# Second-layer weights of a mixture-of-experts kernel: the low part written by ScalarE and finished by an adding DMA

## The chip, the cores and the metric

The kernel runs on one core of a Trainium2 chip. The metric is the device time in microseconds (us) of one execution. Before the change it is 1175.32 us, the median of 3 runs (1174.71 to 1176.95).

The core has five engines with queues of their own that meet only at semaphores. TensorE (PE) multiplies matrices, VectorE (DVE), ScalarE (ACT) and GpSimd (POOL) do elementwise work, SyncE (SP) issues DMAs. GpSimd's queue can issue DMAs too. All DMAs of the core run on the same 16 DMA engines.

## The reference

Three stages, one after the other, on 2304 tokens of 512 features. In short:

```python
x = attention(q, k, v)                    # 4 x 8 heads, 576 positions, local and strided masks
# first mixture: each token goes to one of 8 experts, at most 288 tokens an expert
for e in range(8):
    h = np.maximum(x[mask_e] @ w1[e], 0.0)
    out[mask_e] = h @ w2[e]
# second mixture: all 4 experts on every token, weighted by p
for e in range(4):
    h = np.maximum(x @ v1[e], 0.0)
    y += p[:, e:e + 1] * (h @ v2[e])
```

`w1` and `v1` are the first-layer weights (512 x 1024 for an expert), `w2` and `v2` the second-layer weights (1024 x 512). The experts of the first mixture are filled greedily, in the order of the gate's logits, which the kernel finds by a search.

## The kernel before, in words

Every product is taken three times: a number is split into a high part (rounded to fp32r) and a low part (what the rounding left), and the kernel adds high x high, high x low and low x high. So each weight needs a high tile `wh` and a low tile `wl = raw - wh`.

The program has three stages: attention (to about 140 us of the profiled execution), the routing stage (`steps`, to about 660 us), in which the eight routed experts and a part of the second mixture run interleaved while the search for the next expert's tokens goes on beside them, and the rest of the second mixture (`fast`, to the end). The change touches the routing stage alone.

The weights of the routing stage come in 136 chunks of 128 hidden columns. A chunk has two halves: a = 0 holds 512 x 128 of the first layer, a = 1 holds 128 x 512 of the second layer; each is 128 partitions x 512 floats (256 KB). A chunk passes these places:

- `load` (L841, L842): SP's queue issues one DMA per half into a `raw` tile. There are 8 such tiles, so 4 chunks; a tile is taken again when its last reader is done. SP's queue is in order.
- `prep_hi` (L867): ACT casts both halves to `wh`, some 4 steps ahead of the chunk's first use. `wh` and `wl` have slots for 8 chunks.
- `split_lo` (L875): one subtraction per half writes `wl`. It is recorded under L769 where DVE does it, since DVE's calls pass through a helper there, and under L875 where POOL does it: POOL takes the second halves of chunks 1 to 7 and some of the last chunks, when the search (`chains`) is over.
- `l1` and `l2` (L994): a step is 12 matmuls of the first layer, and 6 or 12 of the second layer, which come two steps later (`LK`). In between, ACT writes `hh = relu(h)` (L887), and DVE writes `hl` (L889, under L769).

The order of instructions is fixed when the program is built. A model called `Pace` counts the time of PE and of DVE; `fill` puts a subtraction of `split_lo` into the program where the model finds DVE free, and `tick` puts the next piece of the search (`chain_a`) or of the gather (`chain_b`) where its inputs should be there. So what DVE has to do decides where these pieces stand in the order of every engine. GpSimd's queue also issues the gathers of the tokens, `xg` (L914), and the scatters of finished rows, `out_dram` (L1090); both wait for DVE.

Of the kernel before, what the change touches and what calls it, by code (L numbers as in the profile page):

```python
# [22 lines left out]
AF = mybir.ActivationFunctionType  # L23
OP = mybir.AluOpType
# [715 lines left out]
NRAW = 4  # L740
# [32 lines left out]
def experts(tc, ident, hot, K, L, xd, side, w1, w2, v1, v2, out, hold, deferred):  # L773
    nc = Pace(tc.nc)
    D, F = 512, 1024
    with ExitStack() as st:
# [22 lines left out]
        for s, S in enumerate(steps):  # L799
            c = chunks[S["ch"]]  # L800
            c.setdefault("first", s)
            c["last"] = s
        for k, c in enumerate(chunks):
            lo = chunks[k - NSLOT]["last"] + 2 + LK if k >= NSLOT else 0
# [3 lines left out]
        plain = len(chunks)  # L808
# [4 lines left out]
        R = [dict() for _ in range(8)]  # L813
        done_l1 = [False] * 8
        state = {"load": 0, "prep": 0, "lo": 0}
# [12 lines left out]
        def load(k):  # L828
            c = chunks[k]
            raw = c["raw"] = [mp.tile([128, 512], FT, name="raw", bufs=2 * NRAW) for _ in range(2)]  # L830
            fc = c["fc"]
            if "m1" in c:
                g = c["m1"]
                ev = ereg[g]
                s1 = w1[bass.ds(ev, 1), :, fc * 128:fc * 128 + 128].rearrange("o (c p) f -> p (o c) f", p=128)
                s2 = w2[bass.ds(ev, 1), fc * 128:fc * 128 + 128, :].rearrange("o p d -> p (o d)")
            else:
                e = c["e"]
                s1 = v1[e, :, fc * 128:fc * 128 + 128].rearrange("(c p) f -> p c f", p=128)
                s2 = v2[e, fc * 128:fc * 128 + 128, :]  # L840
            nc.sync.dma_start(raw[0].rearrange("p (c f) -> p c f", c=4), s1)  # L841
            nc.sync.dma_start(raw[1], s2)  # L842

        def loads(need, ahead):
            while state["load"] < len(chunks):
                k = state["load"]
                c = chunks[k]
                if k >= need and k >= state["prep"] + ahead:
                    return
                if "m1" in c and c["m1"] not in ereg:  # L850
                    g = c["m1"]
                    if k >= need and "e" not in R[g]:
                        return
                    until(lambda: "e" in R[g])
                    ereg[g] = nc.sync.value_load(R[g]["ei"], min_val=0, max_val=7)
                load(k)
                state["load"] += 1

        def prep_hi(k):
            loads(k + 1, 0)  # L860
            c = chunks[k]
            c["at"] = nc.pe
            c["h"] = mp.tile([128, 1024], FR, name="wh", bufs=NSLOT)
            c["l"] = mp.tile([128, 1024], FR, name="wl", bufs=NSLOT)
            for a in range(2):
                sl = slice(512 * a, 512 * a + 512)
                nc.scalar.copy(c["h"][:, sl], c["raw"][a])  # L867

        def split_lo(pool=False):

            k, a = divmod(state["lo"], 2)
            c = chunks[k]
            sl = slice(512 * a, 512 * a + 512)
            eng = nc.gpsimd if pool or 0 < k < 8 and a or not chains and (a or k % 2) else nc.vector
            eng.tensor_tensor(c["l"][:, sl], c["raw"][a], c["h"].bitcast(FT)[:, sl], OP.subtract)  # L875
            state["lo"] += 1
            if a and "x" in R[0]:
                loads(0, NRAW)

        def fill():  # L880

            while chains and state["lo"] < 2 * min(plain, state["prep"]) and nc.dve <= nc.pe and chunks[state["lo"] // 2]["at"] + HI <= nc.pe:
                split_lo()
# [104 lines left out]
        def until(f):  # L988
            while not f():
                assert chains  # L990
                tick(0.1, "b" in chains)
# [156 lines left out]
        def preps(s, n=None):  # L1148
            while state["prep"] < (n or plain) and chunks[state["prep"]]["prep"] <= s:
                prep_hi(state["prep"])  # L1150
                state["prep"] += 1
            while state["lo"] < 2 * state["prep"]:
                c = chunks[state["lo"] // 2]
                if c["first"] > s + (1 if chains else 0) and (chains or c["prep"] >= s):
                    break
                split_lo()
# [177 lines left out]
        for k in range(PRE):  # L1334
            prep_hi(k)
            state["prep"] += 1
            for a in range(2):
                split_lo(a and k)
# [25 lines left out]
def attention_moe_moe(ctx, tc, q, k, v, wg, w1, w2, dp, v1, v2, out):  # L1364
    nc = tc.nc
    ctx.enter_context(tc.manual_schedule())
    cp = ctx.enter_context(tc.tile_pool(name="c", bufs=1))
    dr = ctx.enter_context(tc.tile_pool(name="dr", bufs=1, space=bass.MemoryType.DRAM))
    ident = cp.tile([128, 128], FT, name="ident")
    hot = cp.tile([128, 512], BF, name="hot")  # L1370
    nc.vector.memset(hot, 1.0)
    make_identity(nc, ident)
    L = cp.tile([128, 18, 8], FT, name="L")
    xd = dr.tile([2304, XW], FT, name="xd")
    side = dr.tile([2304, 8], FT, name="side")
    K = route_consts(nc, cp)
    yp = ctx.enter_context(tc.tile_pool(name="yp", bufs=1))
    ready = (lambda *a: first_best(nc, K, L, *a), lambda *a: first_reach(nc, K, *a), lambda *a: first_count(nc, K, *a))
    hold = lambda: yp.tile([128, 2304], FT, name="hold", bufs=3)
    deferred = []  # L1380
    front(tc, ident, hot, q, k, v, wg, dp, xd, L, ready, hold, deferred)
    experts(tc, ident, hot, K, L, xd, side, w1, w2, v1, v2, out, hold, deferred)
# [26 lines left out]
```

## Time and profile before

| | before |
|---|---|
| median of 3 runs | 1175.32 us |
| profiled execution, its own time | 1175.08 us |
| its span, first to last instruction | 1173.4 us |
| PE busy | 1145.3 us (98%) |
| DVE busy | 837.0 us (71%) |
| ACT busy | 613.8 us (52%) |
| POOL busy | 427.0 us (36%) |
| mean granted clock of TensorE | 0.993 |

An engine's busy time is the time in which one of its instructions ran, and it is a sum over stages with different limits: which engine sets the time is read stage by stage. A busy PE is not PE at its peak, since matmuls overlap. The profiled execution took 1.7 us more than its span, and its own time lies 0.24 us under the median, inside the spread of the runs.

### The profile page before, as it was taken

The page shows a single profiled execution, that of the slowest core. Times are in us where ns is not written, and L with a number is a line of the kernel's source. Part 1 is how long each engine was busy: PE and PEld are TensorE (multiplying, and loading weights), DVE is VectorE, ACT ScalarE, POOL GpSimd, SP SyncE. Part 2 cuts the span into 40 slices and gives each one's busy share as a digit, 9 for nine tenths or more (in the row PEclk, how much of TensorE's full clock was granted, in tenths as well). Part 3 has the DMA queues.
Part 4 walks back from the last instruction along what each step waited for, and adds up shares of the span by engine and source line. Part 5 has one row for each costly group of instructions (what it writes and reads, how often), then busy time and mean ns, then how long its engine had stood idle before and what let it go on. Part 6 is the DMA issues. An engine that isn't in the chain of part 4 may idle for free.

```text
span 1173.4 us, 24536 instructions
## 1 busy us (share of the span) xinstructions
PE 1145.3 (98%) x8845; PEld 1027.8 (88%) x8852; DVE 837.0 (71%) x2253; ACT 613.8 (52%) x1599; POOL 427.0 (36%) x474
## 2 busy tenths in 40 slices
PE   9999799999999999999999999999999999999997
PEld 6876598898998998999999999999898899899996
DVE  6777688787876887867755577776776776676663
ACT  5997455452442433555544555555555555555552
POOL 6453130001001000101105465556756566656652
PEclk9999899999999999999999999999999999999999
DMA  7881665553351533656565333333423333333320
GB/s 179 189 189 18 192 211 160 176 147 91 115 176 55 175 118 93 216 180 203 170 192 181 98 101 104 94 108 102 133 91 108 109 91 108 127 108 106 93 73 36
DMA packets 203387, 152.96 MB, mean 130 GB/s; under 512 B 42584, under 2 KB 169886, under 8 KB 202978
## 3 DMA queue, kind: packets, MB, share of 16 engines
q1 hardware_dynamic: 198946, 140.91, 41.0%
q0 software_dynamic: 4320, 10.49, 2.8%
q8 instruction: 69, 1.13, 0.4%
q14 instruction: 52, 0.43, 0.1%
HBM read 141.77 MB, written 9.58 MB: 129 GB/s over the span
## 4 chain that ended last, share of the span: by engine, by line
PE 81%; DVE 4%; ACT 4%; DMA 3%; issue 3%; POOL 3%; POOLq 0%; SPq 0%; ACTq 0%; DVEq 0%
PE o L994 37%; PE h L994 17%; PE h L1226 9%; PE pa L1226 7%; PE pb L1226 3%; DMA raw<-in_moe_w_dram 3%; ACT pr L213 2%; DVE wl L769 2%; POOL wl L1213 1%; PE pa L620 1%; PE pt L230 1%; POOL out_dram L1090 1%; PE s L194 1%; PE av L250 1%; PE tr L158 1%
## 5 line engine op out<-in xcount | busy, mean ns | idle before, releaser
L769 DVE TENSOR_TENSOR wl<-raw,wh 128x512 fp32r<-128x512 f32 x352 | 269.5, 795 | 5.2 <-ACT wh L867 1.8
L887 ACT ACTIVATE hh<-h 128x256 fp32r<-128x256 f32 (+1 forms) x256 | 100.1, 391 | 269.4 <-PE h L994 196.3
L994 PE MATMUL o<-wh,hh 128*128 128x512 f32 x576 | 226.8, 394 | 1.0 <-ACT y L1072 0.5
L994 PE MATMUL o<-wl,hh 128*128 128x512 f32 x576 | 226.5, 393 | 0.0
L994 PE MATMUL o<-wh,hl 128*128 128x512 f32 x576 | 226.0, 392 | 0.0
L1213 POOL TENSOR_TENSOR wl<-raw,wh 128x512 fp32r<-128x512 f32 x96 | 122.3, 1295 | 197.1 <-ACT wh L1212 165.4
L867 ACT CAST wh<-raw 128x512 fp32r<-128x512 f32 x272 | 160.0, 619 | 61.3 <-DMA raw<-in_moe_w_dram 59.5
L769 DVE SCALAR_TENSOR_TENSOR hl<-h,hh 128x256 fp32r<-128x256 f32 (+1 forms) x256 | 110.0, 430 | 114.5 <-ACT hh L887 113.6
L914 POOL DMA_INDIRECT xg<-xd,idx x24 | 27.7, 1152 | 330.4 <-DVE idx L769 194.5
L994 PEld LDWEIGHTS o<-wh,hl 128*128 128x128 f32 x576 | 108.3, 188 | 23.1
L994 PEld LDWEIGHTS o<-wh,hh 128*128 128x128 f32 x576 | 108.3, 188 | 7.2 <-ACT y L1072 0.7
L994 PEld LDWEIGHTS o<-wl,hh 128*128 128x128 f32 x576 | 108.4, 188 | 5.7
L769 DVE TENSOR_TENSOR wl<-sums,wh 128x512 fp32r<-128x512 f32 x96 | 82.1, 856 | 28.6 <-ACT wh L1199 28.5
L1199 ACT CAST wh<-sums 128x512 fp32r<-128x512 f32 x96 | 59.7, 623 | 81.0 <-POOL sums L1187 57.8
L994 PE MATMUL h<-xh,wh 128*128 128x288 f32 x256 | 76.2, 298 | 0.3 <-ACT xh L891 0.3
L994 PE MATMUL h<-xh,wl 128*128 128x288 f32 x256 | 75.7, 296 | 0.6 <-DVE wl L769 0.6
L994 PE MATMUL o<-hh,wl 128*128 128x288 f32 x256 | 76.2, 298 | 0.0
L994 PE MATMUL o<-hh,wh 128*128 128x288 f32 x256 | 76.1, 297 | 0.0
L994 PE MATMUL h<-xl,wh 128*128 128x288 f32 x256 | 75.8, 296 | 0.1
L994 PE MATMUL o<-hl,wh 128*128 128x288 f32 x256 | 75.5, 295 | 0.0
L994 PE MATMUL h<-y256h,wl 128*128 128x256 f32 x256 | 73.5, 287 | 0.0
L994 PE MATMUL h<-y256l,wh 128*128 128x256 f32 x256 | 73.2, 286 | 0.0
(318 smaller groups left out, 2920.0 us busy)
## 6 DMA issues: line engine op xcount, KB each, us to landing
raw<-in_moe_w_dram SPq DMA_DIRECT2D x464, 256.0 KB
vl<-in_v_dram SPq DMA_DIRECT2D x16, 192.0 KB
ql<-in_q_dram SPq DMA_DIRECT2D x12, 144.0 KB
kl<-in_k_dram SPq DMA_DIRECT2D x12, 144.0 KB
qs<-in_q_dram SPq DMA_DIRECT2D x2, 576.0 KB
ks<-in_k_dram SPq DMA_DIRECT2D x2, 576.0 KB
xd<-y SPq DMA_DIRECT2D x2, 576.0 KB
xd<-hl SPq DMA_DIRECT2D x5, 192.0 KB
```

What stands on the lines that cost most here:

```text
L158: nc.tensor.transpose(p[:, 72 * a:72 * a + 72], src[:, r:r + 2, :].rearrange("p r d -> p (r d)"), ident[:72, :72])
L194: nc.tensor.matmul(out[:rows], lt, rt, start=True, stop=True)
L213: nc.scalar.activation(e[:rows, j, :keys], T["s"][:rows, j, :keys], AF.Exp, scale=-1.0, bias=T["mx"][:rows, j:j + 1], accum_out=T["su"][:r ...
L230: nc.tensor.transpose(p[:keys, rows * j:rows * j + rows], T["p"][:rows, j, :keys], ident[:rows, :rows])
L769: return f(*args, **kw)
L867: nc.scalar.copy(c["h"][:, sl], c["raw"][a])
L887: nc.scalar.activation(hi, src, AF.Relu)
L914: nc.gpsimd.indirect_dma_start(out=xg[:, k, :], out_offset=None, in_=xd, in_offset=bass.IndirectOffsetOnAxis(ap=idx[:, k:k + 1], axis=0))
L994: nc.tensor.matmul(out, a, b, start=start, stop=stop)
L1199: nc.scalar.copy(S["W"][nm][0], src[nm]())
L1213: nc.gpsimd.tensor_tensor(l, r, h.bitcast(FT), OP.subtract)
L1226: mmx = lambda o, a, b, first, lastm, n: (nc.tensor.matmul(o, a, b, start=first, stop=lastm, skip_group_check=True), tick(n / 2315 + 0.009))
```

## The change

In chunks 8 to 135 the second half's low part is made in another way. `prep_hi` now also lets ACT write minus the rounded weights into `wl` (the output is fp32r, so it is rounded as `wh` is), and GpSimd's queue issues a DMA that reads the raw half and adds it to `wl`, in place: raw - wh. `split_lo` skips these 128 halves. First halves, chunks 0 to 7 and the last stage stay as they were.

```diff
@@ prep_hi(k)
             for a in range(2):
                 sl = slice(512 * a, 512 * a + 512)
                 nc.scalar.copy(c["h"][:, sl], c["raw"][a])
+                if added(k, a):
+                    nc.scalar.activation(c["l"][:, sl], c["raw"][a], AF.Copy, scale=-1.0)
+                    nc.gpsimd.dma_start(c["l"][:, sl], c["raw"][a], accum_op=OP.add)
+
+        def added(k, a):
+            return a and 8 <= k < plain
 
         def split_lo(pool=False):
 
             k, a = divmod(state["lo"], 2)
+            if added(k, a):
+                state["lo"] += 1
+                if "x" in R[0]:
+                    loads(0, NRAW)
+                return
             c = chunks[k]
```

Eleven lines are new, so L887 of before is L898 after, L914 is L925 and L994 is L1005.

On GpSimd's queue, from the first gather of the routing stage on (`W` and `tk` are tiles of the search), before:

```order
L709 MEMSET tk 128x224
L914 DMA xg<-xd,idx 96x520 x3
L875 TENSOR_TENSOR wl<-raw,wh 128x512 x7
L914 DMA xg<-xd,idx 96x520 x9
L1089 MEMSET spacer 1x1
L1090 DMA out_dram<-acc,p_3163 2304x512
```

The same place now:

```order
L709 MEMSET tk 128x224
L925 DMA xg<-xd,idx 96x520 x3
L886 TENSOR_TENSOR wl<-raw,wh 128x512 x5
L870 DMA wl<-raw 128x512 x2
L886 TENSOR_TENSOR wl<-raw,wh 128x512
L870 DMA wl<-raw 128x512
L886 TENSOR_TENSOR wl<-raw,wh 128x512
L870 DMA wl<-raw 128x512 x10
L925 DMA xg<-xd,idx 96x520 x3
L870 DMA wl<-raw 128x512 x13
L925 DMA xg<-xd,idx 96x520 x3
```

Between two gathers, where this queue had nothing, there now stand 6 to 29 adding DMAs (L870), 128 in all.

On ScalarE's queue, in the routing stage, before:

```order
L867 CAST wh<-raw 128x512 x2
L887 ACTIVATE hh<-h 128x256
L867 CAST wh<-raw 128x512 x2
L887 ACTIVATE hh<-h 128x256
```

And now:

```order
L867 CAST wh<-raw 128x512 x2
L869 ACTIVATE wl<-raw 128x512
L898 ACTIVATE hh<-h 128x288
L867 CAST wh<-raw 128x512 x2
L869 ACTIVATE wl<-raw 128x512
L898 ACTIVATE hh<-h 128x288
```

One more instruction over a 128x512 half stands between the casts of a step and the next `hh`.

On SP's queue, with what each instruction waits for (DMAHW is a DMA of SP, DMASW one of GpSimd's queue), four loads in the later part of the routing stage, before:

```order
L841 DMA raw<-in_moe_w_dram 128x4x128 [waits DMAHW1_49,DVE_49]
L842 DMA raw<-in_moe_w_dram 128x512 [waits DMAHW2_49,DVE_49]
L841 DMA raw<-in_moe_w_dram 128x4x128 [waits DMAHW3_49,DVE_49]
L842 DMA raw<-in_moe_w_dram 128x512 [waits DMAHW4_49,DVE_49]
```

The same four now:

```order
L841 DMA raw<-in_moe_w_dram 128x4x128 [waits DMAHW1_49,DVE_49]
L842 DMA raw<-in_moe_w_dram 128x512 [waits DMAHW2_49,DMASW5_49,Activation_49]
L841 DMA raw<-in_moe_w_dram 128x4x128 [waits DMAHW3_49,DVE_49]
L842 DMA raw<-in_moe_w_dram 128x512 [waits DMAHW4_49,DMASW6_49,Activation_49]
```

The load of a second half waits for an adding DMA where it waited for DVE.

## Rows read from the trace of the kernel before

**Rows 1.** The page's busy times (us, share of the span, instructions): PE.

```profile
PE 1145.3 (98%) x8845; PEld 1027.8 (88%) x8852; DVE 837.0 (71%) x2253; ACT 613.8 (52%) x1599; POOL 427.0 (36%) x474
```

**Rows 2.** Busy time of each engine in three stretches of the routing stage.

```profile
core 0: us, PE busy (x) PEld busy (x) DVE busy (x) ACT busy (x) POOL busy (x), PEclk, DMA share, GB/s
...
160.00:260.00 100.00, 97.99 (x770) 90.08 (x770) 81.22 (x242) 52.57 (x111) 4.48 (x4) 1.00 0.52 161
260.00:465.00 205.00, 204.03 (x1597) 185.41 (x1596) 155.87 (x490) 75.82 (x171) 15.35 (x17) 1.00 0.39 117
465.00:660.00 195.00, 195.00 (x1426) 185.90 (x1425) 130.07 (x269) 98.35 (x217) 34.24 (x31) 1.00 0.60 182
```

**Rows 3.** What PE waited for, 160 to 660 us (total, times, longest).

```profile
PE pb L931 <- DVE xl L769: 0.9, 1, 0.9
PE pa L620 <- DVE G L769: 0.7, 1, 0.7
PE o L994 <- ACT y L1072: 0.5, 1, 0.5
```

**Rows 4.** The chain that ended last, 180 to 225 us (start, us, what).

```profile
183.21 2.90 DMA raw<-in_moe_w_dram
...
207.28 4.49 DMA raw<-in_moe_w_dram
```

**Rows 5.** Instructions by line on ACT, 465 to 660 us (busy, mean | idle before).

```profile
L867 ACT CAST wh<-raw 128x512 fp32r<-128x512 f32 x116 | 66.7, 618 | 10.7 <-DMA raw<-in_moe_w_dram 10.4
L887 ACT ACTIVATE hh<-h 128x288 fp32r<-128x288 f32 x32 | 13.2, 412 | 47.8 <-PE h L994 47.8
```

**Rows 6.** The same on ACT, 160 to 260 us.

```profile
L867 ACT CAST wh<-raw 128x512 fp32r<-128x512 f32 x64 | 38.6, 620 | 24.0 <-DMA raw<-in_moe_w_dram 23.5
```

**Rows 7.** The same on ACT, 260 to 465 us.

```profile
L867 ACT CAST wh<-raw 128x512 fp32r<-128x512 f32 x78 | 46.2, 619 | 16.9 <-DMA raw<-in_moe_w_dram 16.4
```

**Rows 8.** The same on DVE, 160 to 660 us.

```profile
L769 DVE TENSOR_TENSOR wl<-raw,wh 128x512 fp32r<-128x512 f32 x250 | 167.4, 702 | 0.7
```

**Rows 9.** POOL's instructions in order of time, 7.5 to 11.2 us.

```profile
7.89 0.95 POOL L115 DMA_DIRECT2D wgl<-in_moe_w_gate_dram  x1 [0.31 <-POOL wgl L114]
...
10.70 0.57 POOL L124 DMA_DIRECT2D dpr<-in_moe_domain_probs_dram  x1
```

**Rows 10.** Instructions by line on POOL, 465 to 660 us.

```profile
L875 POOL TENSOR_TENSOR wl<-raw,wh 128x512 fp32r<-128x512 f32 x9 | 12.1, 1369 | 41.3 <-DVE wl L769 38.7 <-ACT wh L867 2.6
L914 POOL DMA_INDIRECT xg<-xd,idx x6 | 8.3, 1385 | 83.3 <-DVE idx L769 82.1 <-issue 1.2
```

**Rows 11.** DMA queues, 465 to 660 us (packets, MB, share of 16 engines).

```profile
q1 hardware_dynamic: 44160, 32.95, 55.5%
q0 software_dynamic: 704, 2.25, 3.6%
```

**Rows 12.** DMA share (tenths) and GB/s in 40 slices of 465 to 490 us.

```profile
DMA  6700840000179649910069716615729996279982
GB/s 188 220 2 7 256 157 0 0 0 0 35 226 330 241 126 321 352 46 0 1 196 358 271 39 201 198 22 146 272 71 256 346 357 204 76 233 352 281 292 88
```

**Rows 13.** What SP's queue waited for, 465 to 660 us.

```profile
SPq L841 <- DVE wl L769: 75.0, 47, 6.3
SPq L842 <- DVE wl L769: 21.2, 21, 3.5
```

**Rows 14.** DMA issues of GpSimd's queue, whole span (count, size, us from issue to landing).

```profile
vs<-in_v_dram POOLq DMA_DIRECT2D x12, 54.0 KB, 5.6
...
xg<-xd,idx POOLq DMA_INDIRECT x24, 4.0
```

## The prediction

> **What bounds the kernel now.** I read the busy times of the page first, then the stretches of the routing stage, then what PE waits for there, and last the DMA queues. PE is busy for 98% of the span [rows 1]. The stretches show where the rest lies: from 160 to 660 us, where all the adding DMAs will lie (counted below), PE is idle for 100 - 97.99 = 2.01 us, then for 205 - 204.03 = 0.97 us, then for nothing [rows 2]. So TensorE at its full clock (granted 1.00 in all three) sets this stage, and no edit beside it can win more than 2.98 us. Of its waits the two longest are for DVE, 0.9 and 0.7 us [rows 3]. What the reader is to see beside this is the DMA share: 0.52, 0.39 and 0.60. It is not idle, and in the last stretch it is the next limit behind PE. SP's queue, which issues the weights, waits there for the reader of a raw tile, and that is DVE's subtraction, 75.0 + 21.2 us in 68 waits [rows 13]. ACT's casts waited for weights in all three stretches, 10.4, 23.5 and 16.4 us, without PE feeling it [rows 5 to 7].
>
> **How many, and where.** There are 272 casts `wh<-raw`, two to a chunk. 64, 78 and 116 of them lie in the three stretches [rows 5 to 7], 258, so 14 (chunks 0 to 6) come before 160 us. Chunk 7 keeps its old way. The adding DMAs are therefore 31, 39 and 58 in the three stretches, 128 in sum.
>
> **What is removed.** 128 subtractions over 128x512. GpSimd did 16 of all 272 before and does 10 in the new order, so DVE loses 122, at 702 ns each [rows 8], 86 us, and GpSimd 6 at 1.37 us [rows 10]. DVE is not what PE waits for, except in the 2.98 us above. This term is between 0 and -2.98 us. I take 0: DVE's search pieces are also moved earlier by the time model, and what waits for them is planned as tightly as before.
>
> **What ACT gets.** 128 instructions over 128x512. No row shows one with a scale on this form; the cast of the same form takes 618 ns [rows 5], `hh` over 288 columns 412 ns, and I take 0.62 us, 79 us in all. The late stretch gets 58 x 0.62 = 36 us on top of 98.35 busy of 195 [rows 2], which is 69%. In a step ACT then does 0.41 + 3 x 0.62 = 2.3 us, and a step lasts about 3.1 us (195 us for 32.95 MB, which is 125.7 halves or 62.8 chunks, [rows 11]). Behind the new instruction stands the next `hh`, which waits for PE anyway, 47.8 us in 32 waits [rows 5]. Cost 0.
>
> **What GpSimd's queue gets.** 128 DMA issues. Plain ones took 0.57 and 0.95 us [rows 9]; 58 in the late stretch are 33 to 55 us on an engine that is busy for 34.24 of 195 [rows 2]. Cost 0 as work. Each issue waits for ACT, and behind it stand the gathers `xg`; they are issued long before PE transposes them. The other way round an adding DMA can stand behind a gather that waits for DVE's `idx`, three gathers of 1.39 us each time [rows 10], 4.2 us for one chunk in seven places; the cast of a chunk comes 4 to 5 steps ahead and its second layer two steps late, so `wl` is needed some 6 x 3.1 = 19 us later. Cost 0, and at most what the ring below charges.
>
> **What the 16 DMA engines get.** This is the term that decides. In the late stretch the share of 0.60 leaves 195 x 0.40 = 78 us of all 16 engines [rows 2], for 58 adds: 1.34 us each. No row shows an adding DMA, so I bound it by copies. The software queue moved 2.25 MB in 3.6% of 195 us, 7.0 us [rows 11], which is 0.82 us for the 0.262 MB of a half. A raw load costs 0.555 x 195 / 125.7 = 0.86 us by the same sum. If an add costs as much as one copy, 58 x 0.82 = 48 us fit into 78. If it costs two, since it reads the raw half and what it adds to, 58 x 1.64 = 95 us are 17.1 us too many. If it costs three, because it also writes, 58 x 2.46 = 143 us are 65 too many. From 160 to 260 us the engines have 48 us left, and 31 adds take 25, 51 or 76: 0, 2.8 or 28 us too many. From 260 to 465 us 125 us are left, and even three copies (96) fit.
>
> But share is not capacity. The best slices of the stretch from 465 to 490 us moved up to 358 GB/s at a share of 0.9 or more [rows 12], which is 0.73 us a half. At that rate the loads and the rest of the late stretch (35.2 MB) take 98 us and 58 adds of two copies 85, together 183 of 195. So two copies cost between 0 and 17.1 + 2.8 = 19.9 us. I take two copies as the nearest reading of "read, read, write", and half way between the rates, 10 us.
>
> The Trainium skill's page "Collectives: The Full Stack", section "The bandwidth ceiling: the fold count and why AG ≠ RS ≠ AR", holds that an add in the DMA path reads two sources on the same ring and runs at about half the rate of a copy (a ratio of 1.93 there). No run here shows it yet. By it an add is 1.93 x 0.82 = 1.58 us (an estimate), and the late stretch is 58 x 1.58 - 78 = 13.6 us over.
>
> **What the ring of raw tiles gets.** A second half used to go back to SP after DVE's subtraction. Now it goes back when the add has landed, and SP's queue is in order, so a late one also holds the first half of the next chunk. The trip is now: two casts and the new instruction, 1.86 us; issue to landing, 4.0 us for the gathers and 5.6 us for the plain DMAs of a busier time [rows 14]; one more copy's time for the second operand, 0.82; and the next load's landing, 2.90 to 4.49 us [rows 4]. That is 9.6 to 12.8 us against the 4 x 3.1 = 12.4 us in which the ring turns. At the low end it costs nothing, at the high end 0.4 us in each of 58 / 4 turns, 6 us. I take 3.
>
> **The sum.** 10 + 3 + 0 = 13 us on the profiled execution's 1175.08 us, which is 0.24 us under the median of the runs: 1188 us. Its own range goes from 1178 us (almost all of it fits) to 1204 us (19.9 + 6 + 3 for casts that hold up `hh` in the queue of ACT).
>
> **The rivals.**
>
> *A: hidden, no change.* An add costs about one copy, or the engines find the capacity of their best slices, and PE still sets the stage: 1175 us. For it: 78 us free in the late stretch, PE's leads of several steps, ACT's waits for weights that cost PE nothing. Against it: two operands to read.
>
> The Trainium skill's page "DMA: Bandwidth & Descriptors", section "Anatomy of one DMA — SWDGE (gpsimd) path", puts a DMA at 2.0 us plus its bytes over 436 GB/s. By that rule a half moves in 0.60 us (an estimate), loads and adds would fill little more than half of the late stretch, and the time would stay at 1175 us. The trace disagrees so far: no slice of rows 12 is above 358 GB/s, and a load costs 0.86 us.
>
> *B: faster.* As A, and a lighter DVE gives PE its waits back: at most the 2.98 us, 1172 us. It decides only if nearly all of it comes back, since 2.35 us (0.2%) is about what a measurement of this kernel can tell from no change. For it: the longest waits are on DVE. Against it: they are 1.6 us of the 2.98 [rows 3], and the search is still there.
>
> *C: far slower.* An add costs three copies or more, and from 1.34 us an add on the DMA engines set the late stretch: 65 + 28 = 93 us, 1268 us. For it: nothing in the trace bounds an add from above. Against it: a copy already reads and writes once.
>
> **How the numbers follow.** The forecast has 0.42, A 0.30, B 0.12, C 0.16. Faster by over 0.2% is B, 0.12; within 0.2% is A, 0.30; slower is the forecast and C, 0.58. The range goes from B's 1172 us to 1212 us, a little over the forecast's own end, and leaves out most of C.
>
> **What the profile after would show.** Right: PE idle time appears from 465 to 660 us and little from 260 to 465; that DMA share rises from 0.60 to 0.9 or more; ACT's casts wait for raw far more than 10.4 us; SP's loads of second halves wait for GpSimd's adding DMAs. DVE's subtractions fall by 122, and the last stage from 660 us on keeps its 513 us. The price of an add is read from the software queue's share: 1.64 us of 16 engines for each if I am right, about 0.82 in A and B, 2.46 or more in C. The forecast is wrong if PE stays full while that share is high (the capacity was there), or if PE waits for `wl` itself rather than through late casts.

## The result, and the profile after

The changed kernel takes 1193.34 us (median of 4 runs, 1188.3 to 1198.14) against 1175.4 us before (4 runs): a ratio of 1.0147, 95% interval 1.0122 to 1.0172, so 17 to 18 us slower. The profiled execution took 1188.3 us, the fastest of the four, with a span of 1186.4 us.

First the page of the kernel after: busy times, DMA queues (packets, MB, share of 16 engines), and the groups that changed.

```profile
PE 1150.7 (97%) x8852; PEld 1031.3 (87%) x8852; DVE 766.5 (65%) x2131; ACT 676.0 (57%) x1727; POOL 525.7 (44%) x596
q0 software_dynamic: 22752, 44.06, 19.8%
...
L870 POOL DMA_DIRECT2D wl<-raw x128 | 110.1, 860 | 299.7 <-ACT wl L869 140.8
L769 DVE TENSOR_TENSOR wl<-raw,wh 128x512 fp32r<-128x512 f32 x230 | 192.1, 848 | 8.8 <-ACT wh L867 2.5
L869 ACT ACTIVATE wl<-raw 128x512 fp32r<-128x512 f32 x128 | 80.7, 630 | 0.0
```

DVE lost 122 subtractions (352 before, 230 now) and 70 us of work, ScalarE and GpSimd got 62 and 99 us more [rows 1]. The software queue's share gives the price of an add. Before, it was 2.8% of the span for the same gathers and loads:

```profile
q0 software_dynamic: 4320, 10.49, 2.8%
```

(0.198 x 1186.4 - 0.028 x 1173.4) / 128 = 1.58 us of all 16 engines for one half. That is two copies by the prediction's count (1.64 us).

The windows of the kernel after answer to [rows 2]. The late stretch is taken to 672 us:

```profile
160.00:260.00 100.00, 92.03 (x720) 83.51 (x720) 71.55 (x234) 58.63 (x123) 31.48 (x35) 0.97 0.90 214
260.00:465.00 205.00, 200.59 (x1569) 183.62 (x1568) 130.67 (x450) 92.00 (x207) 43.74 (x52) 0.99 0.68 166
465.00:672.00 207.00, 204.44 (x1468) 194.05 (x1467) 97.80 (x193) 137.17 (x292) 72.34 (x85) 1.00 1.05 258
```

PE's idle time grew from 2.01 to 7.97 us in the first stretch, from 0.97 to 4.41 in the second, and from nothing to 2.56 in the third: 12.0 us more, of which 9.4 come before 465 us. The reader should set this beside the DMA share. Where it is highest, 1.05, PE lost least for its length. The loss is early.

The last stage begins 16.3 us later than before. Laid over the old one with that offset it is the same, as its first 100 us show, before and after:

```profile
660.00:760.00 100.00, 99.54 (x636) 90.47 (x636) 74.31 (x128) 56.37 (x136) 57.03 (x56) 1.00 0.34 102
676.30:776.30 100.00, 99.54 (x637) 90.50 (x636) 74.21 (x128) 56.35 (x136) 57.02 (x56) 1.00 0.34 102
```

So the routing stage got 16.3 us longer. 12.0 of them are idle time of PE. In the other 4.3 us PE was busy, for the same work; the lower clock below is the likely reason.

PE's waits from 155 to 300 us in the kernel after (total, times, longest) say for what:

```profile
PE pa L620 <- DVE G L769: 5.5, 3, 3.2
PE pb L942 <- DMA xg<-xd,idx: 3.6, 3, 2.6
PE o L1005 <- DVE hold L769: 2.0, 1, 2.0
PE pa L627 <- DVE junk L769: 1.5, 1, 1.5
```

L620 and L627 are matmuls of the search, L942 turns the gathered tokens. From 465 to 672 us there is no matmul of L620 or L627: the last expert's search is done. The late stretch has only the gathers' waits (`PE pb L942 <- DVE xl`, 2.6 us).

The chain of waits of the kernel after shows how an add reaches the search (start, us, what):

```profile
163.22 4.24 DMA wl<-raw
...
167.52 2.66 DMA raw<-in_moe_w_dram
...
170.73 0.30 ACT wl L869
...
171.26 0.40 ACT hh L898
171.68 0.46 DVE hl L769
172.14 2.45 DVE wl L769
...
174.70 0.20 DVE th L769
174.93 0.57 DVE G L769
...
175.54 0.64 PE pa L620 x9
```

Read it from the top. The add takes 4.24 us to land. Only then SP may load a later half into that raw tile, 2.66 us more. ScalarE's cast of that chunk stands in its queue ahead of the `hh` of a chunk long computed, so `hh` is late. DVE's `hl` waits for `hh`, and behind `hl` in DVE's queue stand the search's `d`, `th` and `G`, for which PE waits. No wait for `wl` itself is among PE's waits of this stage.

SP's loads wait for adds all through the early stretch, from 160 to 300 us, and those of first halves (L841) more than those of second halves:

```profile
SPq L841 <- DMA wl<-raw: 65.2, 18, 20.5
SPq L842 <- DMA wl<-raw: 27.9, 14, 5.2
```

In sum that is no more than before, when these loads waited for DVE's subtraction (73.9 and 22.2 us from 155 to 300 us). What hurts is the single late load ahead of the search.

One piece of the chain is no wait. The subtraction `wl` at 172.14 us is a single one, and GpSimd makes one of the subtractions that it keeps at the same time:

```profile
172.06 2.54 DVE L769 TENSOR_TENSOR wl<-raw,wh 128x512 fp32r<-128x512 f32 x1
172.49 1.54 POOL L886 TENSOR_TENSOR wl<-raw,wh 128x512 fp32r<-128x512 f32 x1
```

It takes 2.54 us where the median one of this stage takes 0.68. Before, GpSimd began the last of its early subtractions at 161.55 us; now two of them stand behind adds in its queue. That they are what slows DVE here was not tested by itself.

The second place is the gather. POOL's instructions in order of time, after:

```profile
206.00 0.85 POOL L870 DMA_DIRECT2D wl<-raw  x1 [3.34 <-PE pa L627]
207.15 0.99 POOL L925 DMA_INDIRECT xg<-xd,idx  x1 [0.30 <-DVE d L769]
```

and before:

```profile
204.33 0.91 POOL L914 DMA_INDIRECT xg<-xd,idx  x1 [41.27 <-DVE idx L769]
```

Before, the gather went out as soon as DVE had written `idx`. Now DVE writes `idx` here:

```profile
200.94 0.15 DVE L769 CAST idx<-pb 96x3 int32<-96x3 f32 x1
```

It is ready at 201.09 us, but the queue stands at an add that waits for ScalarE, and the gather starts at 207.15, 6.1 us later. (The releasers in brackets name what ended last by the profile; an add needs ScalarE's `wl`, which for the add at 206.00 us ended at 205.71.)

The stalls have an echo. The granted clock, 1.00 throughout before [rows 2], fell in three pieces of the kernel after, each a few us behind stalls of PE:

```profile
165.00:180.00 15.00, 10.62 (x81) 10.05 (x80) 11.11 (x29) 5.38 (x11) 5.82 (x6) 0.89 0.92 220
215.00:230.00 15.00, 14.58 (x101) 12.60 (x101) 8.15 (x26) 8.93 (x20) 2.50 (x3) 0.89 0.79 173
270.00:290.00 20.00, 18.02 (x130) 16.35 (x129) 11.63 (x43) 8.31 (x24) 2.51 (x3) 0.91 0.77 191
```

In each piece the clock stood for a part of the time at the lower of its two levels (1.2 GHz, half of 2.4). 0.89 of 15 us and 0.91 of 20 us are 1.7 to 1.8 us of work each, 5.1 us at most in all three; 4.3 us is what PE's busy time grew by.

One thing must be known to compare the two profiled executions. The last pieces of the chain, before and after:

```profile
1165.97 1.21 POOLq L1404
```

```profile
1182.11 1.19 POOLq L1415
```

After these the span before ended at 1173.4 us, 6.2 us later, and the span after at 1186.4 us, 3.1 us later. So the work was 16.1 us behind where the spans differ by 13.0. Of the experiments below, e1, e5, e6, e9 and e10 have the long tail in their profiled execution (6.2 to 6.5 us), the others the short one (3.1 to 3.9 us). Whether it goes with the kernel or with the execution no run shows, so a difference of two totals across this line may be off by some 3 us as a measure of the routing stage.

### The profile page after: what moved, and what is told of

Its sections match the earlier page's. It is cut to its first block, busy times and chain, and to the rows that moved or that the text cites. A ratio compares the mean times of both kernels' runs of the same rounds, so it can differ in the third digit from the quotient of the medians.

```text
span 1186.4 us, 24976 instructions
## 1 busy us (share of the span) xinstructions
PE 1150.7 (97%) x8852; PEld 1031.3 (87%) x8852; DVE 766.5 (65%) x2131; ACT 676.0 (57%) x1727; POOL 525.7 (44%) x596
## 3 DMA queue, kind: packets, MB, share of 16 engines
q0 software_dynamic: 22752, 44.06, 19.8%
## 4 chain that ended last, share of the span: by engine, by line
PE 84%; DMA 4%; issue 3%; ACT 3%; DVE 3%; POOL 3%; SPq 0%; POOLq 0%; DVEq 0%; ACTq 0%
PE o L1005 37%; PE h L1005 18%; PE h L1237 9%; PE pa L1237 7%; PE pb L1237 3%; DMA raw<-in_moe_w_dram 2%; ACT pr L213 1%; PE pt L230 1%; POOL wl L1224 1%; DMA wl<-raw 1%; PE pa L620 1%; DMA xg<-xd,idx 1%; PE s L194 1%; PE av L250 1%; PE av L243 1%
## 5 line engine op out<-in xcount | busy, mean ns | idle before, releaser
L870 POOL DMA_DIRECT2D wl<-raw x128 | 110.1, 860 | 299.7 <-ACT wl L869 140.8
L898 ACT ACTIVATE hh<-h 128x256 fp32r<-128x256 f32 (+1 forms) x256 | 99.6, 389 | 235.1 <-PE h L1005 163.4
L1005 PE MATMUL o<-wh,hh 128*128 128x512 f32 x576 | 226.7, 394 | 2.0 <-DVE hold L769 2.0
L1005 PE MATMUL o<-wl,hh 128*128 128x512 f32 x576 | 227.0, 394 | 0.0
L1005 PE MATMUL o<-wh,hl 128*128 128x512 f32 x576 | 226.9, 394 | 0.0
L769 DVE TENSOR_TENSOR wl<-raw,wh 128x512 fp32r<-128x512 f32 x230 | 192.1, 848 | 8.8 <-ACT wh L867 2.5
L1005 PEld LDWEIGHTS o<-wh,hl 128*128 128x128 f32 x576 | 108.6, 189 | 22.7
L1005 PEld LDWEIGHTS o<-wh,hh 128*128 128x128 f32 x576 | 108.7, 189 | 8.1 <-issue 2.2
L1005 PEld LDWEIGHTS o<-wl,hh 128*128 128x128 f32 x576 | 108.7, 189 | 6.0
L769 DVE TENSOR_TENSOR wl<-sums,wh 128x512 fp32r<-128x512 f32 x96 | 78.8, 822 | 30.8 <-ACT wh L1210 30.6
L869 ACT ACTIVATE wl<-raw 128x512 fp32r<-128x512 f32 x128 | 80.7, 630 | 0.0
L1005 PE MATMUL o<-hh,wl 128*128 128x288 f32 x256 | 76.6, 299 | 0.0
L1005 PE MATMUL h<-xh,wh 128*128 128x288 f32 x256 | 76.4, 298 | 0.1
L1005 PE MATMUL o<-hl,wh 128*128 128x288 f32 x256 | 76.4, 298 | 0.0
L1005 PE MATMUL h<-xh,wl 128*128 128x288 f32 x256 | 75.8, 296 | 0.6 <-DVE wl L769 0.6
L1005 PE MATMUL o<-hh,wh 128*128 128x288 f32 x256 | 76.2, 297 | 0.0
L1005 PE MATMUL h<-xl,wh 128*128 128x288 f32 x256 | 75.8, 296 | 0.0
L1005 PE MATMUL h<-y256h,wl 128*128 128x256 f32 x256 | 74.2, 290 | 0.0
```

The source lines that it names most:

```text
L769: return f(*args, **kw)
L869: nc.scalar.activation(c["l"][:, sl], c["raw"][a], AF.Copy, scale=-1.0)
L870: nc.gpsimd.dma_start(c["l"][:, sl], c["raw"][a], accum_op=OP.add)
L898: nc.scalar.activation(hi, src, AF.Relu)
L1005: nc.tensor.matmul(out, a, b, start=start, stop=stop)
```

## The experiments

In the expectations, H is the theory that a raw tile comes back late, and the gather goes out late, because an add takes long to land; C that the work on the 16 DMA engines delays other transfers; O that the new order of PE and DVE, made by the time model, costs the time. Differences of two kernels are taken from their ratios times 1176 us, or from the medians where both were measured side by side. By the intervals of the table such a difference is open by 2 to 5 us either way.

| run | what is in it | median, us | before, us | ratio (95% interval) |
|---|---|---|---|---|
| e1_late | adds from chunk 40 on | 1183.35 | 1176.5 | 1.0059 (1.0039 to 1.0079) |
| e2_early | adds in chunks 8 to 39 | 1188.11 | 1176.5 | 1.0099 (1.0060 to 1.0138) |
| e3_order | all adds, old order | 1206.9 | 1176.5 | 1.0254 (1.0215 to 1.0293) |
| e4_hbm | adds read HBM where they can | 1185.37 | 1176.5 | 1.0071 (1.0051 to 1.0090) |
| e5_act | before + ScalarE's copies | 1183.72 | 1176.56 | 1.0060 (1.0043 to 1.0076) |
| e6_pool | GpSimd subtracts | 1188.51 | 1176.56 | 1.0101 (1.0084 to 1.0118) |
| e7_copy | plain copies for adds | 1181.97 | 1176.56 | 1.0060 (1.0038 to 1.0082) |
| e8_defer | adds issued later | 1188.99 | 1176.56 | 1.0100 (1.0084 to 1.0117) |
| e9_order_only | new order, old work | 1180.0 | 1176.6 | 1.0029 (1.0018 to 1.0041) |
| e10_order_act | + ScalarE's copies | 1182.69 | 1176.6 | 1.0052 (1.0038 to 1.0065) |
| e11_tiny | + DMAs of 8 KB in place of adds | 1186.93 | 1175.97 | 1.0087 (1.0073 to 1.0101) |
| e12_aside | + their full work, nobody waits | 1198.43 | 1175.97 | 1.0194 (1.0180 to 1.0208) |

**e1_late and e2_early: where.** One line each, the second with `8 <= k < 40`; the other halves go back to DVE and are charged in the model.

```diff
-            return a and 8 <= k < plain
+            return a and 40 <= k < plain
```

> Adding DMAs only in chunks 40 to 135; chunks 8 to 39 keep DVE's subtraction. 97 adds are left, 58 of them in the late stretch, where the share of the DMA engines was over 1.0. Theory H (hand-back: in the first 120 us of the routing stage weights and one gather come late, because raw tiles come back only when an add has landed and because the gather stands behind adds on GpSimd's queue; the late stretch absorbs the adds): 1175 to 1180 us, PE idle under 2 us from 160 to 300 us beyond the kernel before. Rival C (capacity: the 16 DMA engines are too full, worst in the late stretch): at least 1185 us. Rival O (order: the search pieces were moved by the time model, which hurts wherever it is): between the two, about 1188 us times the share of moved pieces, with PE waiting for DVE's search results and not after weights.

> Adding DMAs only in chunks 8 to 39; the 96 later second halves keep the subtraction. H: nearly the whole loss, 1187 to 1195 us, with 32 adds of 128. Rival C: under 1180 us, since only 32 adds of 1.6 us are left, 2.8 us too many by the forecast's own sum. Rival O: some 1180 to 1185 us.

32 adds in the early chunks cost 1.0099, 96 later ones (not 97) 1.0059. An early add costs about five times a late one (11.6 / 32 = 0.36 us against 6.9 / 96 = 0.07). H holds for the early ones, and C and O fall there. The late ones are not free: H, which had them at 1180 us or less, missed by 3 us.

**e3_order: the order.** All adds, but the time model charges DVE as if it subtracted. PE's order is then that of before.

```diff
             if added(k, a):
                 state["lo"] += 1
+                if chains:
+                    nc.dve = max(nc.dve, nc.pe) + 0.15 + 512 / 960
```

> All 128 adds, but the time model still charges DVE for the subtractions that are gone, so PE's instruction order is that of the kernel before, word for word. H: 1188 to 1198 us as after the change, since tiles come back as late; gathers stand in the same place relative to PE as before, so the gather may hurt less (down to 1184). Rival C: 1193 us. Rival O: 1175 to 1178 us, since the order is the old one.

12.6 us slower than the change, not faster. O falls with the opposite sign: with adds in it, the new order saves time. H and C, which had asked for no more than 1198 us, missed it too. PE's waits of this run from 155 to 672 us, the longest rows:

```profile
PE o L1007 <- ACT y L1085: 9.2, 3, 4.3
PE pb L944 <- DMA xg<-xd,idx: 5.5, 3, 4.9
```

A wait for ScalarE's `y` that cost 0.5 us before [rows 3] is now 9.2 us. `y` stands in ScalarE's queue with the casts; ahead of the longest of these waits a cast waited 2.67 us for its weights.

**e4_hbm: the raw tile comes back earlier.** The adds of second-mixture chunks read the weights from HBM again, so the raw tile is free when ScalarE has read it.

```diff
-                    nc.gpsimd.dma_start(c["l"][:, sl], c["raw"][a], accum_op=OP.add)
+                    nc.gpsimd.dma_start(c["l"][:, sl], c["raw"][a] if "m1" in c else v2[c["e"], 128 * c["fc"]:128 * c["fc"] + 128, :], accum_op=OP.add)
```

> The adds of the second mixture's chunks (24 of the 32 in chunks 8 to 39, 72 in all) read the raw weights from HBM again instead of the raw tile, so this tile comes back as soon as ACT has read it; adds of routed chunks as after the change. Bytes and adds are the same. H: the waits of ACT for weights from 160 to 300 us fall from 19.8 us to under 10, and the time to 1178 to 1186 us; what the gather costs stays. Rival C: 1193 us or more, since HBM is read more. Rival O: 1193 us.

8.9 us of the 17 come back (0.0076 x 1176). SP's loads wait for adds for 38.0 us from 160 to 300 us, where it was 93.1. The casts' wait for weights there falls from 19.8 to 13.6 us, less than H asked; the gather's wait stays, at 4.0 us. The hand-back is a part, not all.

The sum of the casts' waits is a poor measure, though. The kernel before has more of it, from 160 to 300 us, than the change:

```profile
L867 ACT CAST wh<-raw 128x512 fp32r<-128x512 f32 x73 | 43.8, 619 | 24.3 <-DMA raw<-in_moe_w_dram 23.8
```

What PE feels is which cast comes late, and what stands behind it, not how long the casts wait in all.

**e5_act: ScalarE's instruction alone.** The kernel before, with the negated copies, which DVE then overwrites. The order is the old one.

```diff
                 nc.scalar.copy(c["h"][:, sl], c["raw"][a])
+                if a and 8 <= k < plain:
+                    nc.scalar.activation(c["l"][:, sl], c["raw"][a], AF.Copy, scale=-1.0)
```

> The kernel before, with one thing added: ACT's 128 negated copies into the low half, which DVE or GpSimd then overwrites by the subtraction of before. No add, the order on PE and DVE of before. If ACT's 0.63 us a chunk ahead of the next relu cost something by itself: 1178 us or more, with PE waiting for the relu. Theory H (the adds hold raw tiles, and the gathers stand behind them) and rival C (the DMA engines' capacity): 1174 to 1177 us, no change.

7.2 us slower, with no add. PE is idle for 6.4 us from 160 to 300 us, where it was 2.4 before. PE's waits of this run from 155 to 380 us:

```profile
PE pa L620 <- DVE G L769: 3.0, 3, 1.3
...
PE o L996 <- ACT y L1074: 2.0, 1, 2.0
```

The expectation had asked for a wait of PE for the relu. PE's long waits are for the search and for `y`, which stands in ScalarE's queue as the relu does.

**e6_pool: no add, no copy.** GpSimd subtracts where the adds were issued, in the new order.

```diff
-                    nc.scalar.activation(c["l"][:, sl], c["raw"][a], AF.Copy, scale=-1.0)
-                    nc.gpsimd.dma_start(c["l"][:, sl], c["raw"][a], accum_op=OP.add)
+                    nc.gpsimd.tensor_tensor(c["l"][:, sl], c["raw"][a], c["h"].bitcast(FT)[:, sl], OP.subtract)
```

> In place of negated copy and adding DMA, GpSimd subtracts (1.3 us each), at the same place of the program and in the order of after the change. Result as in the reference. No add on the DMA engines; a raw tile comes back 1.3 us after its cast instead of 4 to 6. H: the waits of PE for late weights from 160 to 300 us go, the time is 1173 to 1178 us, below or at the kernel before, since DVE has 122 subtractions less; the gather may still stand behind a subtraction that waits for ACT. Rival C: 1173 to 1176 us as well. If the new order by itself were harmful: over 1182 us.

H missed by 10 us. The time is that of the last reading (over 1182 us, the new order harmful), but the run brought a cost of its own, which the row of DVE's own subtractions shows, from 160 to 300 us in this run:

```profile
L769 DVE TENSOR_TENSOR wl<-raw,wh 128x512 fp32r<-128x512 f32 x34 | 28.5, 843 | 0.0
```

In the change 34 of them take 734 ns each. So the run isolates neither the add nor the order.

**e7_copy: half the price.** A plain copy of the raw half into `wl` in place of the add; the low part is left out. Queue, waits and hand-back stay.

```diff
-                    nc.gpsimd.dma_start(c["l"][:, sl], c["raw"][a], accum_op=OP.add)
+                    nc.gpsimd.dma_start(c["l"].bitcast(FT)[:, sl], c["raw"][a])
```

> The adding DMAs become plain copies of the same bytes, so the low part of these halves is left out (it holds the raw weights). Order, ACT's work, queues and tiles as after the change. It asks what the adding itself costs: the share of the software queue should fall from 1.58 us of 16 engines for a half to about 0.82. H: the tile comes back about 0.8 to 1 us earlier, so 1183 to 1190 us. Rival C: most of the loss goes, 1175 to 1180 us. If not the price but the path over GpSimd's queue costs: 1190 us or more.

Its software queue and its issues on the page:

```profile
q0 software_dynamic: 14560, 44.06, 10.7%
L870 POOL DMA_DIRECT2D wl<-raw x128 | 69.6, 544 | 328.4 <-ACT wl L869 197.3
```

A copy costs (0.107 x 1179.4 - 0.028 x 1173.4) / 128 = 0.73 us, against 1.58 for an add, and 10.2 us of the 17 go with it, give or take 4. The result lies between H and C: the price on the engines matters, by itself or through the landing time. GpSimd's issue is shorter here too, 544 ns against 860.

**e8_defer: the gather first.** The add is issued where DVE's subtraction would have stood, later in GpSimd's queue.

```diff
-                    nc.gpsimd.dma_start(c["l"][:, sl], c["raw"][a], accum_op=OP.add)
...
             if added(k, a):
                 state["lo"] += 1
+                c = chunks[k]
+                nc.gpsimd.dma_start(c["l"][:, 512:], c["raw"][a], accum_op=OP.add)
```

> All adds and the order on PE and DVE as after the change, but an add is issued where DVE's subtraction of that half would have stood, later in GpSimd's order, so that ACT's negated copy is done by then and the gathers wait less behind adds. H: the wait of PE for the gather near 211 us (3.6 us) falls under 1.5 us, while raw tiles come back later, so SP's waits for adds from 160 to 300 us grow; in sum 1188 to 1200 us. Rival C: 1193 us, unchanged.

PE's waits from 155 to 300 us:

```profile
PE pb L943 <- DVE xl L769: 3.8, 1, 3.8
...
PE pb L943 <- DMA xg<-xd,idx: 0.3, 1, 0.3
```

The wait for the gather's DMA is gone (3.6 to 0.3 us), and 5.5 us were won in the total, as H had it. But a new wait of 3.8 us stands at the same matmuls, for DVE's `xl`. The casts wait 28.0 us for weights instead of 19.8, while SP's waits for adds fell from 93.1 to 83.8 us, though H had asked that they grow.

**e9 to e12: the change built up in steps.** These start from the new order with the work of before (DVE subtracts, uncharged; it also takes the 6 late halves that GpSimd had), and add one thing each. The diffs are cut to the lines that matter.

```diff
# e9: no copies, no adds
             if added(k, a):
+                was = nc.dve
+                nc.vector.tensor_tensor(c["l"][:, 512:], c["raw"][a], c["h"].bitcast(FT)[:, 512:], OP.subtract)
+                nc.dve = was
...
# e10: and ScalarE's copies
+                    nc.scalar.activation(c["l"][:, sl], c["raw"][a], AF.Copy, scale=-1.0)
...
# e11: and a small DMA in the place of the add
+                    nc.gpsimd.dma_start(scr[k % 8][:, :4], c["h"].bitcast(FT)[:, 512:516])
...
# e12: full size in place of e11's (chunks 8 to 15 without accum_op)
...
+                        nc.gpsimd.dma_start(scr[k % 8], c["h"].bitcast(FT)[:, 512:], accum_op=OP.add)
```

> No negated copies and no adds: DVE makes all 128 low parts where the changed kernel only counts them, and the time model doesn't charge them. PE's order is that of the changed kernel, DVE has the work of before. Theory (the new order is lighter by itself, and without it the adds cost about 13 us more, as the run with the old order and all adds showed): if the gain lies in the order, this kernel is at or under the kernel before, 1165 to 1175 us, and beats both. Rival (the gain lies in DVE being free of the 128 subtractions, and the new order asks DVE for pieces earlier than it can deliver them): 1178 to 1190 us, with PE waiting for DVE's search tiles from 160 to 300 us.

> As the run with the new order alone, and ScalarE also writes the 128 negated copies, which DVE then overwrites: no adds. Theory (each instruction that stands before a relu on ScalarE's queue delays the chain behind it): 5 to 9 us above the run with the new order alone, as the negated copies in the old order cost about 7 us. Rival (ScalarE has room in the new order, and what costs is the add): within 2 us of the run with the new order alone.

e9: 3.4 us slower than before, so the new order is no gain by itself; the theory missed, and the rival's range holds. Its window of 160 to 260 us has PE at 95.76 (97.99 before):

```profile
160.00:260.00 100.00, 95.76 (x783) 87.33 (x782) 88.13 (x275) 48.73 (x102) 10.40 (x7) 1.00 0.56 161
```

DVE's 88.13 of 100 (81.22 before) shows what the order does: it asks DVE for more, earlier. e10: 2.7 us more for ScalarE's copies, between the two theories, and less than the 7.2 us in the old order. In e10 to e12 DVE's subtraction must also wait for the copy that it overwrites (2.9 us in 8 waits in e10, from 155 to 465 us), which the change doesn't have.

> As the run with the new order and the negated copies, DVE makes the low parts; and GpSimd's queue issues, where the adds stand, a DMA of 16 bytes a partition from the high tile to DRAM, which waits for ScalarE's cast as the add does. Nobody waits for it, and it moves 8 KB. What is left of the adds is their place in GpSimd's queue ahead of the gathers. Theory G (the gather behind the adds costs much): 3 to 6 us above the run without it, and PE waits for the gather's tokens between 205 and 220 us by 3 us or more. Rival (what costs is the time an add takes to land): within 1.5 us of that run.

> As the run with the 8 KB DMAs, but the DMA is full size: it adds the 128x512 high half to a tile in DRAM (the first eight are plain copies). The 16 DMA engines have the work of 120 adds, the queue has its place, but neither the low parts nor the raw tiles wait for an add. Theory H (the raw tile that comes back only when the add has landed is most of what is left): within 3 us of the run with the 8 KB DMAs. Rival C (the work on the 16 DMA engines delays the loads): 5 us or more above it, with casts that wait for raw tiles from 160 to 300 us by 15 us or more.

e11: 4.1 us more (0.0035 x 1176), as G said; in the profiled executions, with their two tails, the last work ends 10.2 us later than in e10. PE's waits from 155 to 300 us:

```profile
PE pa L620 <- DVE G L769: 5.0, 5, 2.4
PE pb L946 <- DMA xg<-xd,idx: 3.8, 3, 1.9
```

Both great stalls of the change are there without an add; in e10 these rows are 2.0 and 1.4 us. The second is the gather. How the first arises shows in the chain of this run:

```profile
163.82 0.54 POOL scr L871
164.37 1.31 POOL wl L890
165.70 2.78 DMA raw<-in_moe_w_dram
...
169.56 0.40 ACT hh L902
```

GpSimd's own subtraction for one of the first chunks (`wl`, L890) stands behind a DMA that waits for ScalarE, so its raw tile comes back late. It is the path of the chain shown for the change, with the queue in the place of the add.

e12: 11.5 us more than e11, though no engine is seen to wait for an add. Its first window, its casts from 160 to 300 us, and three pieces of its chain:

```profile
160.00:260.00 100.00, 89.54 (x674) 79.97 (x673) 77.74 (x242) 54.43 (x114) 25.21 (x30) 0.95 0.80 198
```

```profile
L868 ACT CAST wh<-raw 128x512 fp32r<-128x512 f32 x66 | 39.5, 618 | 36.1 <-DMA raw<-in_moe_w_dram 34.2 <-issue 1.6
```

```profile
193.59 3.92 DMA raw<-in_moe_w_dram
...
198.00 3.57 DMA raw<-in_moe_w_dram
...
202.33 4.27 DMA raw<-in_moe_w_dram
```

Three loads in a row stand on the chain, and ScalarE's casts wait 34.2 us (19.9 in e11, 23.8 before). Here C is right: the adds' work on the DMA engines delays the loads, at a mean share of 0.80, while no engine waits for an add. What e12 doesn't separate is how much of this is due to its adds ending in DRAM and not in SBUF, and to GpSimd, whose issues take 0.85 us (median) where e11's take 0.54.

## Why the prediction was right and wrong

The forecast of 1188 us, slower, held in direction, and 1193.34 us lies in the forecast's own range, 1178 to 1204 us. By its steps it was right for a part of the reasons.

**Price of an add: right.** Two copies, 1.64 us, predicted; 1.58 us measured. Rival C (2.46 us or more) falls by this row, rivals A and B by the time. In e7_copy a copy of the same half costs 0.73 us, so an add is 1.58 / 0.73 = 2.2 copies. The Trainium skill's page "Collectives: The Full Stack", section "The bandwidth ceiling: the fold count and why AG ≠ RS ≠ AR", puts a reduce step, which reads two sources, at half the rate of a copy; that page measured 1.93 in a ring of several cores, and 2.2 here is a little worse. The Trainium skill's page "DMA: Bandwidth & Descriptors", section "Anatomy of one DMA — SWDGE (gpsimd) path", has the linear rule by which a half would move in 0.60 us (an estimate). Both 0.73 and 1.58 us are above it, but they are sums of packet times, in a share that can pass 1.0, and do not settle that rule.

**Where the DMA engines' work is paid: wrong.** This step failed. "In the late stretch the share of 0.60 leaves 78 us" made an overflow there the main term. The late stretch took a share of 1.05 and left PE 204.44 of 207 us. By the prediction's own test ("PE stays full while that share is high") the capacity was there. The time was lost at 160 to 300 us, where the sum had found 2.8 us over. Not the sum of the work decides but how late a single load lands, and who stands behind the cast that waits for it; e12_aside shows such a delay at a mean share of 0.80. Of the signs named for the late stretch, SP's loads of second halves did wait for adds (68.5 us in 33 waits), but the casts waited 14.5 us, not far more than 10.4. The size was near: 10 us were predicted, and e7_copy takes back 10.2 us with the cheaper DMA. That is luck in part, for the working was about another place.

**ScalarE, cost 0: wrong.** The duration was right (0.63 against 0.62 us). But "behind the new instruction stands the next `hh`, which waits for PE anyway" was read in the late stretch [rows 5] and used for all. In the stretch with the search the same instruction costs PE: 7.2 us over the whole kernel in the old order (e5_act), 2.7 us in the new one (e10_order_act).

**GpSimd's queue, cost 0: wrong.** "They are issued long before PE transposes them": the gather went out 6.1 us after its `idx`, and PE waited 3.6 us. With the subtractions that GpSimd keeps in the first chunks, which the prediction did not see behind the adds, the place in the queue costs 4.1 us (e11_tiny).

**The ring, 3 us: too small.** Giving the tile back early brought 8.9 us (e4_hbm), though that edit changes more than the hand-back, since its adds read HBM. The trip as predicted was right in kind: the chain shows 4.24 us for the add's landing and 2.66 for the next load. But the ring does not turn in four chunks any more. In the program after, 40 of the 264 loads take a tile that a half two or three chunks earlier held, where it was 1 before; the load on the chain, of chunk 10's second half, takes the tile of chunk 8's.

**DVE, 0: right in sign.** No wait was given back. But the new order isn't "planned as tightly as before": alone it costs 3.4 us (e9_order_only). It pays only when DVE is really relieved: with all adds in it, it saves 12.6 us (e3_order).

**The last stage: right.** It takes 510.1 us from 676.3 us on, against 513.4 from 660 us on before, and the 3 us between them are the tail.

**The clock: not in the sum.** The prediction took the full clock of before and charged nothing for it. Behind the stalls came three pieces with a lower one, and PE's busy time for the same work grew by 4.3 of the 16.3 us.

The steps do not add up to 17.3 us as a plain sum: 3.4 (order), 2.7 (ScalarE), 4.1 (queue) make 10.2 us in e11_tiny, and the change itself is 7 us above that, with the adds' work and hand-back in and DVE's 122 subtractions out. Of these 7 us the runs do not split work on the engines, hand-back and relief exactly. A deeper ring of raw tiles was not tried. None of the kernels beats the one before.

## What to carry to other kernels

Ask of each added instruction and DMA not whether its engine or the DMA engines have room on average, but which in-order queue it stands in, and what latency-bound chain stands behind it there; here the search for the next expert's tokens set the price of what was put ahead of it. An adding DMA cost about two copies here and handed its source back only when it had landed. Moving elementwise work to it won nothing at any place that was tried: even the 96 late adds cost 6.9 us. And read a cover ("it waits anyway") in the stretch in which the edit lies, not in the one with the largest sum.

## What the runs showed of the hardware

- An adding DMA of a 128x512 half costs 1.58 us of all 16 engines, a copy of the same half 0.73 us; GpSimd is busy for 860 ns to issue the one, 544 ns for the other.
- The DMA share of a stretch went to 1.05 at 258 GB/s, with PE at 204.44 of 207 us: the share sums packet times and isn't a ceiling.
- DVE's subtraction of a half takes 843 ns in the mean beside GpSimd's subtractions (e6_pool), 734 ns in the change and 688 ns before, each from 160 to 300 us; the longest one of the change, beside a subtraction of GpSimd, took 2.54 us.
- The granted clock fell to 0.89 to 0.91 in three pieces of 15 to 20 us, each behind stalls of PE, where before it stayed at 1.00 from 160 to 660 us; PE's busy time for the same work grew by 4.3 us.
